# Retention by batch and head pair with tiled fp32 matmuls, and routing through an on-chip slot table

## The chip, the cores and the metric

One core of one Trainium2 chip. The metric is the device time of one execution in microseconds (us). The kernel before takes 367.27 us (median of 3 runs, 363.37 to 367.58); its profiled execution has a span of 363.7 us. Profiles say which state an execution was in; comparisons below are between fast ones unless a sentence says otherwise.

## The reference

```python
# q, k, v: (4 batches, 8 heads, 768 tokens, 64), fp32
state = zeros((B, H, D, D))
for t in range(S):
    state = gamma[h] * state + outer(k[:, :, t], v[:, :, t])
    y[:, :, t] = scale * (q[:, :, t] @ state)
x = y.transpose(0, 2, 1, 3).reshape(3072, 512)

skip_score = x @ w_skip                 # only rows with a score over 0 go to an expert
e_idx  = argmax(x @ w_gate)             # one of 8 experts
gate_w = softmax(x @ w_gate)[e_idx]
out = x
out[active] = x + gate_w * (relu(x @ w1[e]) @ w2[e])   # w1: 512x1024, w2: 1024x512 for each expert
```

For the inputs of this case 1510 of the 3072 rows are active, 133 to 229 per expert.

## The kernel before

Retention works on chunks of 128 tokens, a pair of heads at a time: transposes of q and k, scores, mask, values, and a running state. The two heads of a pair are kept apart by padding K and V with zeros to 128 columns, so every fp32 pass uses the whole array.

```python
    for r in range(SROWS // 128):                    # the scatter buffer is zeroed
        nc.scalar.dma_start(out=xs[r * 128 : (r + 1) * 128, :], in_=xsinit[:, :])
    ...
    def stage_D(s):                                  # scores of two heads, and the state product
        ...
        nc.tensor.matmul(out=ps[:, 0:128], lhsT=KT0z[r][:, :], rhs=QTs[s][:, :], start=True, stop=True)
        nc.tensor.matmul(out=ps[:, 128:256], lhsT=KT1z[r][:, :], rhs=QTs[s][:, :], start=True, stop=True)
        nc.tensor.matmul(out=ps[:, 256:384], lhsT=kg[j][:, pcs], rhs=va[j][:, pcs], start=True, stop=True)
    ...
    def gate_b(j):                                   # 24 times: rows of a chunk go to the buffer
        ...
        nc.gpsimd.indirect_dma_start(
            out=xs[:, :], out_offset=bass.IndirectOffsetOnAxis(ap=dest_i[:, 0:1], axis=0),
            in_=xt[j][:, 0 : XSW], ...)
    ...
    def issue_w2(e, fb, eng):                        # weights: fp32 staging tile, cast by VectorE
        w2st = poolW.tile([128, DM], FP32, tag="w2st", bufs=2, name="w2st")
        nc.sync.dma_start(out=w2st[:, :], in_=moe_w2[e, fb * 128 : (fb + 1) * 128, :])
        ...
        eng.tensor_copy(wbf[:, :], w2st[:, :])
    ...
    # per expert: read 256 rows of xs, transpose, two layers, and for each 128 rows
            nc.gpsimd.indirect_dma_start(
                out=out[:, :], out_offset=bass.IndirectOffsetOnAxis(ap=toks[e][st][:, 0:1], axis=0),
                in_=yout[:, :], ...)
```

## Time and profile before

| stage | us | what sets it |
|---|---|---|
| start | 0 to 30 | ScalarE's queue sits in the issue of the zeroing writes |
| retention and gating | 30 to 254 | TensorE, 87% filled with passes of 0.11 us |
| hole | 254 to 280 | last blocks are gated and routed |
| experts | 280 to 364 | second-layer weights, and at the end the scatters |

In the lines of the profile PE is TensorE, PEld its weight loads, DVE VectorE, ACT ScalarE, POOL GpSimd, SP SyncE. A pass is one weight load with the matmul that uses it; an fp32 matmul takes two passes, an fp32 transpose one. PSUM is the memory that TensorE writes its results to, in banks.

The prediction shows the slices, windows, waits and groups that carry this. One more view is needed to understand what came: GpSimd's last instructions in the order of time (start, duration, instruction, and in brackets how long the engine stood before it and for what):

```profile
348.52 0.97 POOL L463 DMA_INDIRECT out_dram<-yout,tok_i  x1 [3.14 <-DVE yout L459]
352.03 0.97 POOL L463 DMA_INDIRECT out_dram<-yout,tok_i  x1 [2.54 <-DMA out_dram<-yout,tok_i]
355.09 0.97 POOL L463 DMA_INDIRECT out_dram<-yout,tok_i  x1 [2.09 <-DMA out_dram<-yout,tok_i]
358.60 0.97 POOL L463 DMA_INDIRECT out_dram<-yout,tok_i  x1 [2.54 <-DMA out_dram<-yout,tok_i]
```

The reader is to see that each of the last three scatters waits for the scatter before it, and that they stand about 3.4 us apart. In this kernel that binds only at the very end; earlier the scatters come further apart anyway. The prediction did not use these lines, and it should have.

### The profile page before, as it was taken

Reading aid. Unit: us, or ns where it says so; the run is one execution under the profiler, and the core shown is the slowest. Engines: PE = TensorE matmul, PEld = TensorE weight load, DVE = VectorE, ACT = ScalarE, POOL = GpSimd, SP = SyncE. Lnnn points to the kernel's source line nnn. Section 1 sums busy time; section 2 is a strip of 40 time slices with the busy share of each in tenths; the row PEclk is TensorE's granted clock in tenths of the full one; section 3 lists DMA queues with packets and bytes.
Section 4 is the critical chain, followed back from the end, with each engine's and each line's share of the span. In section 5 each row is a group of like instructions: output and inputs, shape, how many; then the busy total and the mean of one; then the engine's idle time right before and its main releaser. Section 6 shows DMA issues by size and latency. Waiting matters only on the chain. (4 is left out here: it accounts for less than half of the span.)

```text
span 363.7 us, 7487 instructions
## 1 busy us (share of the span) xinstructions
PE 298.8 (82%) x2192; PEld 242.4 (67%) x2192; DVE 204.9 (56%) x896; ACT 222.4 (61%) x977; POOL 137.1 (38%) x309
## 2 busy tenths in 40 slices
PE   0005999999999999999999999999524999999860
PEld 0003988888888888888788888888313666666530
DVE  1011667878887878877777777877520224333330
ACT  4006699888887888778778878884102444444310
POOL 8600344545554351454455444441031112222222
PEclk9999999999999999999999999999655999999996
DMA  7999678799969897894987788785416167676611
GB/s 175 263 318 329 190 202 237 220 279 284 240 214 267 241 299 194 239 283 144 234 226 210 204 232 234 214 238 191 142 61 199 45 229 233 228 244 207 205 62 50
DMA packets 101303, 77.31 MB, mean 213 GB/s; under 512 B 79386, under 2 KB 79386, under 8 KB 101264
## 3 DMA queue, kind: packets, MB, share of 16 engines
q1 hardware_dynamic: 95616, 62.96, 61.8%
q0 software_dynamic: 3200, 9.41, 6.9%
q10 hardware_dynamic: 2448, 4.47, 3.7%
q8 instruction: 17, 0.28, 0.3%
q14 instruction: 22, 0.18, 0.2%
HBM read 56.66 MB, written 21.28 MB: 214 GB/s over the span
## 5 line engine op out<-in xcount | busy, mean ns | idle before, releaser
L206 POOL TENSOR_SCALAR kg_all<-k_all,gamk 128x64 f32<-128x64 f32 x192 | 85.6, 471 | 56.6 <-PE atkv_ps L234 27.4
L200 ACT ACTIVATE qg_all<-q_all,gamq 128x64 f32<-128x64 f32 x192 | 55.1, 340 | 21.8 <-DMA xs<-xsinit 21.1
L348 POOL DMA_INDIRECT xs<-x_tile,dest_i x24 | 25.0, 1043 | 96.8 <-ACT QT L220 21.6
L212 PE MATMUL tqk_ps<-ident,qg_all 128*128 128x128 f32 x96 | 28.9, 301 | 30.4 <-ACT V0z L223 30.2
L240 DVE TENSOR_TENSOR ATm<-atkv_ps,maskp 128x256 f32<-128x256 f32 x96 | 40.3, 420 | 21.9 <-PE atkv_ps L234 18.7
L171 DVE CAST w2bf<-w2st 128x512 bf16<-128x512 f32 x64 | 27.7, 434 | 38.5 <-DMA w2st<-in_moe_w_dram 38.3
L446 ACT ACTIVATE hT_sb<-hT_ps 128x256 bf16<-128x256 f32 x64 | 24.5, 384 | 31.8 <-PE hT_ps L441 27.6
L164 DVE CAST w1bf<-w1st 128x512 bf16<-128x512 f32 x64 | 25.5, 437 | 29.9 <-DMA w1st<-in_moe_w_dram 29.9
L232 PE MATMUL atkv_ps<-QT,KT0z 128*128 128x128 f32 x192 | 40.9, 296 | 0.6 <-ACT KT0z L221 0.3
L263 PE MATMUL Y_ps<-V0z,ATm 128*128 128x128 f32 x192 | 38.7, 284 | 1.3 <-DVE ATm L240 1.3
L233 PE MATMUL atkv_ps<-QT,KT1z 128*128 128x128 f32 x192 | 39.2, 287 | 0.0
L234 PE MATMUL atkv_ps<-v_all,kg_all 128*128 128x128 f32 x192 | 39.1, 286 | 0.0
L264 PE MATMUL Y_ps<-V1z,ATm 128*128 128x128 f32 x192 | 37.9, 280 | 0.0
L212 PEld LDWEIGHTS tqk_ps<-ident,qg_all 128*128 128x128 f32 x96 | 13.8, 144 | 35.3 <-issue 31.9
L271 ACT COPY x_tile<-Y_ps 128x128 f32<-128x128 f32 x96 | 25.5, 266 | 19.4 <-PE Y_ps L266 14.3
L441 PE MATMUL hT_ps<-xTe,w1bf 128*128 128x256 bf16 x256 | 35.1, 275 | 0.8
L463 POOL DMA_INDIRECT out_dram<-yout,tok_i x16 | 15.8, 985 | 51.5 <-DMA out_dram<-yout,tok_i 18.7
L441 PEld LDWEIGHTS <-w1bf 128*128 128x128 bf16 x256 | 25.2, 98 | 11.1 <-issue 5.0
L232 PEld LDWEIGHTS atkv_ps<-QT,KT0z 128*128 128x128 f32 x192 | 30.0, 197 | 3.0 <-ACT KT0z L221 2.3
L263 PEld LDWEIGHTS Y_ps<-V0z,ATm 128*128 128x128 f32 x192 | 29.8, 196 | 2.7 <-DVE ATm L240 1.6
L454 PE MATMUL y_ps<-w2bf,hT_sb 128*128 128x512 bf16 x128 | 30.1, 379 | 1.5 <-DVE yout L459 1.5
L291 PE MATMUL gps<-xT_sb,Wc 128*9 128x128 f32 x192 | 29.4, 280 | 2.1 <-DVE xT_sb L279 2.1
(89 smaller groups left out, 641.5 us busy)
## 6 DMA issues: line engine op xcount, KB each, us to landing
w1st<-in_moe_w_dram SPq DMA_DIRECT2D x32, 512.0 KB
w2st<-in_moe_w_dram SPq DMA_DIRECT2D x64, 256.0 KB
q_all<-in_q_dram SPq DMA_DIRECT2D x24, 256.0 KB
k_all<-in_k_dram SPq DMA_DIRECT2D x24, 256.0 KB
v_all<-in_v_dram SPq DMA_DIRECT2D x24, 256.0 KB
out_dram<-x_tile SPq DMA_DIRECT2D x24, 256.0 KB
xs<-xsinit ACTq DMA_DIRECT2D x17, 257.0 KB
xg<-xs SPq DMA_DIRECT2D x16, 257.0 KB
```

Of the source, the lines that this page charges most:

```text
L200: nc.scalar.activation(out=qg[j][:, hc], in_=qa[j][:, hc], func=AF.Copy, bias=0.0, scale=gamq[:, h : h + 1])
L206: nc.gpsimd.tensor_scalar(kg[j][:, hc], ka[j][:, hc], gamk[:, h : h + 1], None, ALU.mult)
L212: nc.tensor.transpose(out=ps[:, 0:128], in_=qg[j][:, pcs], identity=ident[:, :])
L232: nc.tensor.matmul(out=ps[:, 0:128], lhsT=KT0z[r][:, :], rhs=QTs[s][:, :], start=True, stop=True)
L233: nc.tensor.matmul(out=ps[:, 128:256], lhsT=KT1z[r][:, :], rhs=QTs[s][:, :], start=True, stop=True)
L234: nc.tensor.matmul(out=ps[:, 256:384], lhsT=kg[j][:, pcs], rhs=va[j][:, pcs], start=True, stop=True)
L240: nc.vector.tensor_tensor(out=sb[:, :], in0=at_ps[s][:, 0:256], in1=maskp[p][:, :], op=ALU.mult)
L263: nc.tensor.matmul(out=yp[:, 0:128], lhsT=ATm[s][:, 0:128], rhs=V0z[r][:, :], start=True, stop=False)
L264: nc.tensor.matmul(out=yp[:, 0:128], lhsT=ATm[s][:, 128:256], rhs=V1z[r][:, :], start=False, stop=(c == 0))
L291: nc.tensor.matmul(out=gps[0:9, 0:128], lhsT=Wc[:, db * 9 : db * 9 + 9], rhs=xT_sb[:, db * 128 : (db + 1) * 128], start=(db == 0), stop=(d ...
L441: nc.tensor.matmul(out=hT_ps[:, 0:CAP], lhsT=w1bf[e][db][:, fb * 128 : (fb + 1) * 128], rhs=xTes[e][:, db * CAP : (db + 1) * CAP], start=( ...
L454: nc.tensor.matmul(out=y_ps[:, :], lhsT=hTs[fb][:, st * 128 : (st + 1) * 128], rhs=w2bf[e][fb][:, :], start=(fb == 0), stop=(fb == NFB - 1),)
```

## The change

The intent: fewer and cheaper passes in retention, no zeroing, no scatter buffer in memory, no staging and casting of weights. One unit is a batch and a head pair (16 of them, 768 tokens). Partition p of the q and k tiles holds tokens 6p to 6p+5, so that a row is one run of 1536 bytes; GpSimd scales q and k of a whole unit by one multiplication each. Scores use 64 rows of the array for each head, values and state 64 columns, so that two heads can run side by side. Row numbers of each expert's slots are built on chip by small matmuls with one-hot columns, rows are gathered from the output, weights are cast by the DMA itself, and a loop would take over if an expert got more than 256 rows (here it runs zero times). The diff cut to its core:

```diff
-        nc.scalar.dma_start(out=xs[r * 128 : (r + 1) * 128, :], in_=xsinit[:, :])
...
-        nc.sync.dma_start(out=qa[j][:, :], in_=q[b, :, t0 : t0 + C, :].transpose([1, 0, 2]))
+        nc.sync.dma_start(out=qw[i][:, :, :], in_=q[b, hs].rearrange("h (p r) d -> p h (r d)", p=128))
...
-            nc.gpsimd.tensor_scalar(kg[j][:, hc], ka[j][:, hc], gamk[:, h : h + 1], None, ALU.mult)
+            G_.tensor_tensor(o[:, :, :, :], w[i][:, :, :].rearrange("p h (r d) -> p r h d", d=D), sc, ALU.mult)
...
+        o = dst[i][:, :].rearrange("p (t r) -> p r t", r=R)[:, a * HB : (a + 1) * HB, :]
+        A_.copy(out=o, in_=ps[:, :].rearrange("p (r t) -> p r t", r=HB))
...
-        nc.tensor.matmul(out=ps[:, 0:128], lhsT=KT0z[r][:, :], rhs=QTs[s][:, :], start=True, stop=True)
-        nc.tensor.matmul(out=ps[:, 128:256], lhsT=KT1z[r][:, :], rhs=QTs[s][:, :], start=True, stop=True)
+                hp = slice(64 * h, 64 * h + 64)
+                PE.matmul(out=ps[h][:, r * C : (r + 1) * C], lhsT=KT[i][hp, cs], rhs=QT[i][hp, cs], start=True, stop=True)
...
+                PE.matmul(
+                    out=KV[i][64 * h : 64 * h + 64, c * D : (c + 1) * D],
+                    lhsT=Kn[i][:, c, 64 * h : 64 * h + 64], rhs=vn[i][:, h, c, :], start=True, stop=True,
+                )
...
-        nc.sync.dma_start(out=w2st[:, :], in_=moe_w2[e, fb * 128 : (fb + 1) * 128, :])
-        eng.tensor_copy(wbf[:, :], w2st[:, :])
+            G_.dma_start(out=w2b[e][:, :, :], in_=moe_w2[e].rearrange("(a p) d -> p a d", p=128))
...
+    for e in range(E):
+        gather(e, gi)                       # 16 indirect row loads, 128 rows each
+    for e in range(NEARLY, E):              # NEARLY = 4
+        load_w(e, 0, poolE)
+        load_w(e, 1, poolE)
...
+            yo = poolE.tile([128, DM], FP32, tag="yo", bufs=4, name="yo")
+            V_.scalar_tensor_tensor(
+                out=yo[:, :], in0=ps[:, :], scalar=g[:, st, e : e + 1], in1=xg[e, st][:, :], op0=ALU.mult, op1=ALU.add
+            )
+            G_.indirect_dma_start(
+                out=out[:, :], out_offset=bass.IndirectOffsetOnAxis(ap=si[:, st, e : e + 1], axis=0), ...
...
+    NPASS = (N + CAP - 1) // CAP - 1
+    thr_i = poolE.tile([128, NPASS], I32, tag="thr_i", bufs=1, name="thr_i")
+    G_.iota(thr_i[:, :], pattern=[[CAP, NPASS]], base=CAP, channel_multiplier=0)
+    V_.tensor_copy(thr[:, :], thr_i[:, :])  # the test for overflow, once, after all experts
```

> **What bounds the kernel now.** I read four views in this order: the 40 slices of the page, to cut the span into stages; a table of busy time by stretch; the waits; the groups of instructions.
>
> ```profile
> PE   0005999999999999999999999999524999999860
> PEclk9999999999999999999999999999655999999996
> GB/s 175 263 318 329 190 202 237 220 279 284 240 214 267 241 299 194 239 283 144 234 226 210 204 232 234 214 238 191 142 61 199 45 229 233 228 244 207 205 62 50
> ```
>
> Each slice is 9.1 us. Four stages show: no matmul for three slices, 24 full ones (retention and gating), a hole of three slices with a lower clock (the last blocks are routed and scattered), then the experts.
>
> ```profile
> core 0: us, PE busy (x) PEld busy (x) DVE busy (x) ACT busy (x) POOL busy (x), PEclk, DMA share, GB/s
> 100.00:150.00 50.00, 48.84 (x401) 43.60 (x400) 40.66 (x192) 40.85 (x189) 22.63 (x44) 1.00 0.83 243
> 265.00:290.00 25.00, 14.21 (x79) 9.45 (x80) 3.74 (x17) 6.19 (x18) 3.85 (x9) 0.67 0.30 98
> 320.00:363.00 43.00, 29.57 (x184) 17.73 (x182) 12.55 (x24) 13.16 (x37) 10.23 (x13) 0.92 0.47 153
> ```
>
> Retention is set by PE (48.8 of 50 us), though DVE and ACT stand at 41 and the DMA engines at 0.83. In the last 43 us nothing is full: PE 29.6, DMA 0.47. The waits say why, and why the start is empty:
>
> ```profile
> DVE w2bf L171 <- DMA w2st<-in_moe_w_dram: 38.3, 30, 3.4
> PE tqk_ps L212 <- ACT V0z L223: 30.2, 1, 30.2
> ACT qg_all L200 <- DMA xs<-xsinit: 21.1, 1, 21.1
> POOL out_dram L463 <- DMA out_dram<-yout,tok_i: 18.7, 6, 4.8
> ```
>
> PE's 30.2 us before its first transposes go back to ACT, whose queue sits 21.1 us in the issue of 17 zeroing writes of the scatter buffer (4.4 MB) that compete with the first loads. At the end, second-layer weights arrive through two staging tiles and a DVE cast. Four groups give my unit prices:
>
> ```profile
> L206 POOL TENSOR_SCALAR kg_all<-k_all,gamk 128x64 f32<-128x64 f32 x192 | 85.6, 471 | 56.6 <-PE atkv_ps L234 27.4
> L240 DVE TENSOR_TENSOR ATm<-atkv_ps,maskp 128x256 f32<-128x256 f32 x96 | 40.3, 420 | 21.9 <-PE atkv_ps L234 18.7
> L348 POOL DMA_INDIRECT xs<-x_tile,dest_i x24 | 25.0, 1043 | 96.8 <-ACT QT L220 21.6
> L441 PE MATMUL hT_ps<-xTe,w1bf 128*128 128x256 bf16 x256 | 35.1, 275 | 0.8
> ```
>
> The means of PE are latencies. The price of a pass is its spacing: in the order of time around 154 us, one fp32 matmul of 128 columns starts 0.22 us after the last (two weight-load-and-matmul passes of 0.11), an fp32 transpose takes 0.11, eight first-layer bf16 matmuls take 0.9 plus a wait of 0.2, and 14 second-layer ones 3.02 us, 0.216 each.
>
> **What the Trainium skill says.** "TensorE: Matmul & The Clock Gate", Back-to-back issue gap, gives N/2.4 + 2.5 ns warm, 216 ns for 512 columns; the trace has 216. Its Part 3 (Packing small matmuls) measures 3.07x for four row tiles running at once at 512 columns. The kernel before pads K and V with zeros and uses no tile, so its trace neither agrees nor disagrees. "GPSIMD Engine Reference", 3.1, puts a two-input elementwise operation at about 2.6 cycles per element and 4497 ns for 2048, 1.7 us for 768; the trace has only a one-input form, 471 ns for 64, mostly fixed. "DMA: Bandwidth & Descriptors", SWDGE vs HWDGE vs iDMA, says that a cast in flight can be issued from GpSimd only. The trace has no cast in flight.
>
> **The change, part by part.**
>
> *Start.* The scatter buffer, its zeroing and 16 zeroed operand tiles go. The first unit needs q and k, 0.79 MB; at the 175 to 263 GB/s of the first slices that is 3 to 4.5 us plus some 2 us of latency. GpSimd then scales q and k, about 2 us each. First transpose near 9 us instead of about 29: minus 20 us.
>
> *Retention on PE.* The count of passes before, per chunk of 128 tokens: 8 transposes, 24 for the two score products and the state, 22.7 for the output, 4 + 8 for gate transposes and logits, 6 for the rest, 72.7 passes, 8.0 us at 0.11. The stage takes 220 us for 24 chunks, 9.2 each, so PE is 87% filled. After, per unit (batch and head pair, six chunks): 12 + 5 + 6 transposes, 24 passes of scores with 64 rows, 20 of state with 64 columns on both sides, 10 with the state, 24 of values with 64 columns: 101. Sixteen units make 1616 against 1744 before. So almost nothing comes from the count; it must come from the 68 tiled passes of a unit overlapping in pairs. Full overlap would halve them; I take 0.08 us instead of 0.11, since each still needs its weight load: 33 x 0.11 + 68 x 0.08 = 9.1 us per unit.
>
> Waits inside a unit: the second half of the scores reuses the same two PSUM banks, so PE waits for two DVE masks (128x256 costs 0.42, so 384 columns about 0.56 each, an estimate): about 1 us. The state sums are 10 small DVE operations of 0.2 us behind the masks and two copies of 0.56; the state product of the unit, only 12 passes of q later, waits about 1 us more. Changes of tile shape: 0.5. Together 2.5, so 11.6 us per unit, 185 for sixteen. Gate logits and rows are 8 matmuls of 384 columns (0.64 each, some overlapped), 12 short passes and the slot table: about 5 us in each of three batches that lie inside, 15.
>
> Other engines per unit: DVE 4 x 0.56 + 2 x 0.56 + 10 x 0.2 = 5.4 us (the weight casts, 53 us in all, are gone); ACT eight copies of 256 to 384 columns at about 0.5, 3.9; GpSimd two scalings of 1.7 to 2.9, at most 5.8, plus descriptors of one weight load every second unit (512 or 1024 rows at the 8 ns per row that the scatter's 1.04 us for 128 rows gives: 4 to 8 us). All under 11.6. DMA moves 18.9 + 16.8 + 6.3 = 42 MB in 200 us, 210 GB/s, with q and k in 1536-byte runs instead of 256: no bound. Retention ends near 9 + 200 + 5 (last unit's output) = 214 us, against 254.
>
> *The hole.* The before needs 20 us from the last output (254) to the first expert row loads (274). After, logits 3, rows and about 15 small DVE operations at 0.2 with four changes of engine 7, table 3, slot arithmetic 2: 15 us; row numbers at about 230. Then a gather, 1.0 to issue and some 2 to land, and the transposes 2: first expert matmul near 235.
>
> *Experts.* PE: 32 first-layer passes of 0.11, now two blocks per bank and so without the 0.2 waits, 16 of 0.216, 8 short transposes: 7.6 us, eight make 61, so 235 + 61 = 296. But weights of experts 4 to 7 (16.8 MB of fp32 read) are issued on GpSimd behind 16 gathers of 1.04 us: from 247 us. At 300 GB/s (the highest slices have 318 and 329, with fewer bytes in a run) they take 56 us, the last lands at 303, the last second layer adds 4 and the last scatter, its landing and the end 5 (before: last issue at 358.6, end 363.7): 312. The DMA chain is then 11 us longer than PE's. Counts per expert here, worked out from the inputs, are 133 to 229, so the overflow loop runs zero times; its test costs perhaps 2 us beside the last scatters. Prediction on the span 312, and runs lie within 1% of the traced span: 312 us.
>
> **The rivals.**
> 1. Tiles do not overlap (sequencer or mode changes bind). Then 101 x 0.11 = 11.1 us and 3 of waits, 14.1 per unit: plus 40, 350 us. For it: every fp32 pass in the trace stands 0.11 apart, even where only 8 columns stream. Against: the skill's 3.07x.
> 2. Tiles overlap fully: 33 x 0.11 + 34 x 0.11 = 7.4 us, and DVE and the waits show; unit of 9.5, 280 us. The trace's weight load latency of 0.2 us per pass speaks against all of it.
> 3. The cast in flight runs below 300 GB/s. At 150, 16.8 MB take 112 us from 247: 368 us, no gain. Nothing in the trace speaks for or against; an expert wait on weights is what it would show. Faster than 300 it is hidden and PE sets 301.
> 4. Scatters stuck behind the weight descriptors in GpSimd's queue: four output tiles and two banks fill after three experts, and PE stops until the queue is free, up to 20 us more.
>
> **Range and chances.** The start is nearly certain (minus 20), the hole minus 5. Rivals 1 and 3 each raise the time by 40 or more and I give each one chance in six or less in that size; rival 2 has about the same. The range is 278 to 348. Slower than 374 takes both 1 and 3. Chances: faster 0.91, same 0.05, slower 0.04.
>
> **What would show it.** First transpose at 8 to 12 us. Units 11 to 12 us apart, with score and value passes under 0.1 us apart and a PE wait for the score masks. First expert matmul at about 235. Experts 0 to 3 at 7 to 8 us, then waits of PE for DMA of the weights. If units take over 13 us, the tiling step is wrong; if the experts' stage is longer than 85 us, the cast's rate or GpSimd's queue is; if GpSimd is busy over 70% of retention, its scaling was mis-sized and sets the pace.

## The result and the profile after

The changed kernel takes 322.36 us (median of 4 runs, 321.98 to 323.18; all fast) against 366.97 us for the kernel before in the same rounds; the ratio is 0.883, 95% interval 0.877 to 0.889. Ratios here and below are those of the record, from fast runs of the same rounds, so not quite the ratio of the medians quoted. The profiled span is 320.4 us.

The slices of the page (8 us each), to be laid beside those of before:

```profile
PE   1897999966999998999999993087995009889200
PEclk9998999995799999999999995569999557999855
GB/s 215 229 198 250 248 217 213 233 209 295 336 237 102 271 213 70 91 149 101 147 3 0 2 84 114 233 250 182 175 210 209 210 141 49 42 66 54 52 74 28
```

TensorE starts in the first slice and retention is over in the 24th, at 188.5 us. There are two stretches without work: the one expected between retention and the experts, and a second one in the slices at 245 to 265 us. After it the memory traffic is near 50 GB/s to the end. The table of busy time by stretch for the steady part of retention, the second stretch and the last 55 us (columns as in the prediction):

```profile
100.00:150.00 50.00, 48.20 (x543) 39.31 (x541) 29.87 (x106) 25.01 (x43) 14.97 (x10) 1.00 0.48 135
245.00:265.00 20.00, 0.71 (x2) 0.25 (x2) 0.75 (x1) 0.34 (x1) 0.75 (x1) 0.58 0.96 175
265.00:320.00 55.00, 30.96 (x192) 18.47 (x190) 10.77 (x18) 7.16 (x12) 13.88 (x15) 0.81 0.14 53
```

In 100 to 150 us TensorE is as full as before (48.2 of 50), while VectorE and ScalarE fell from 41 to 30 and 25. In the last 55 us nothing is full, not even the DMA (0.14). The waits name what is being waited for:

```profile
DVE yo L485 <- DMA out_dram<-yo,si: 48.7, 12, 20.6
POOL out_dram L488 <- DVE yo L485: 38.9, 2, 35.6
POOL qks L181 <- DMA kw<-in_k_dram: 29.3, 4, 13.8
PE yps L480 <- DVE yo L485: 22.0, 4, 19.4
```

VectorE waits for scatters to free its four output tiles, and TensorE stands 19.4 us for VectorE. (The second line blames VectorE for GpSimd's 35.6 us; VectorE was itself waiting for the scatter.) The third line belongs to the first 80 us: GpSimd waits for k. GpSimd's queue, in the order of time:

```profile
198.74 0.81 POOL L162 DMA_DIRECT2D w1b<-in_moe_w_dram  x1 [40.92 <-PE cnt L512]
199.86 1.09 POOL L446 DMA_INDIRECT xg<-out_dram,gi  x1 [0.31 <-issue]
...
226.13 0.98 POOL L165 DMA_DIRECT2D w2b<-in_moe_w_dram  x1
227.42 1.06 POOL L488 DMA_INDIRECT out_dram<-yo,si  x1 [0.30 <-DVE xb L456]
...
264.25 1.05 POOL L488 DMA_INDIRECT out_dram<-yo,si  x1 [35.60 <-DVE yo L485]
...
313.74 0.97 POOL L488 DMA_INDIRECT out_dram<-yo,si  x1 [2.48 <-DMA out_dram<-yo,si]
```

One weight load is issued at 198.7 us, then sixteen gathers and seven more loads from 199.9 to 227 us. The first scatter goes out at 227.4 and the second only at 264.3. From there fifteen scatters are issued 264.3 to 313.7 us: 14 steps in 49.5 us, 3.5 us each. One link of them in the chain that ended last:

```profile
288.87 2.67 DMA out_dram<-yo,si
291.59 0.51 issue
292.09 0.03 POOLq L488
292.12 0.19 issue
292.32 2.57 DMA out_dram<-yo,si
```

Each scatter lands before the next is issued: 2.6 us from the start of its issue (0.97 us of it the issue) to its landing, and 0.7 to 0.8 us of hand-over. In the packed trace's list of semaphores the scatters wait for the one before them; all write to the output, and nothing in the program says that their rows differ. The Trainium skill ("DMA: Bandwidth & Descriptors", Two DMAs through the same engine are not ordered) says that the only order an author has between two transfers is the first one's completion semaphore. That the scheduler takes these writes for overlapping and orders them so is argued here; x_scratch below tests it. The trace agrees with the page in that each scatter is issued only after the landing of the one before, 3.4 to 3.5 us per scatter, as in the last lines of before. The bytes matter little: worked out from the inputs, the fourth scatter writes 5 rows and its step is 2.96 us, and a scatter of 128 rows takes 3.45.

The groups that answer to those of before, busy time and mean duration of one:

```profile
L216 DVE TENSOR_TENSOR ATm<-atps,maskc 128x384 f32<-128x384 f32 x64 | 32.7, 553 | 67.3 <-PE atps L214 67.3
L193 ACT COPY QT<-tps 128x384 f32<-128x384 f32 x32 | 26.0, 863 | 66.6 <-PE tps L191 66.6
L181 POOL TENSOR_TENSOR qks<-qw,tq 128x768 f32<-128x768 f32 x16 | 23.9, 1495 | 61.1 <-PE tps L191 41.1
```

The mask cost what was estimated (0.56), GpSimd's scaling a little less than the lower estimate (1.7), and ScalarE's copy more (863 ns against 489 ns for its contiguous copy of the same shape).

### The profile page after: what moved, and what is told of

Read it like the earlier page. It is cut to its first block, busy times and chain, and to the rows that moved or that the text cites. A ratio compares the mean times of both kernels' runs of the same rounds, so it can differ in the third digit from the quotient of the medians.

```text
span 320.4 us, 5739 instructions
## 1 busy us (share of the span) xinstructions
PE 240.1 (75%) x2253; PEld 183.8 (57%) x2253; DVE 132.5 (41%) x456; ACT 102.5 (32%) x175; POOL 96.0 (30%) x96
## 5 line engine op out<-in xcount | busy, mean ns | idle before, releaser
L216 DVE TENSOR_TENSOR ATm<-atps,maskc 128x384 f32<-128x384 f32 x64 | 32.7, 553 | 67.3 <-PE atps L214 67.3
L480 PE MATMUL yps<-w2b,hT 128*128 128x512 bf16 x128 | 31.3, 396 | 22.0 <-DVE yo L485 22.0
L191 PE MATMUL tps<-ident,qks 128*128 128x128 f32 x192 | 39.7, 304 | 10.7 <-POOL qks L181 6.5
L193 ACT COPY QT<-tps 128x384 f32<-128x384 f32 x32 | 26.0, 863 | 66.6 <-PE tps L191 66.6
L181 POOL TENSOR_TENSOR qks<-qw,tq 128x768 f32<-128x768 f32 x16 | 23.9, 1495 | 61.1 <-PE tps L191 41.1
L214 PE MATMUL atps<-QT,KT 64*128 64x128 f32 x384 | 38.5, 298 | 0.0
L181 POOL TENSOR_TENSOR qks<-kw,tk 128x768 f32<-128x768 f32 x16 | 24.0, 1498 | 39.4 <-DMA kw<-in_k_dram 29.3
L214 PEld LDWEIGHTS atps<-QT,KT 64*128 64x128 f32 x384 | 32.3, 194 | 5.7 <-issue 2.8
L485 DVE SCALAR_TENSOR_TENSOR yo<-yps,g,xg 128x512 f32<-128x512 f32 x16 | 12.0, 750 | 53.8 <-DMA out_dram<-yo,si 48.7
L469 PE MATMUL hps<-xgT,w1b 128*128 128x256 bf16 x256 | 31.5, 281 | 1.7 <-ACT hT L473 1.7
L247 PE MATMUL yps<-QT,Zb 128*128 128x128 f32 x160 | 30.4, 297 | 0.0
L238 DVE TENSOR_TENSOR Zb<-kvps,Zb 64x64 f32<-64x64 f32 x128 | 28.5, 222 | 4.0
L257 PE MATMUL yps<-ATm,vn 128*64 128x128 f32 x384 | 26.9, 280 | 0.0
```

The costliest lines, as they stand in the source:

```text
L181: G_.tensor_tensor(o[:, :, :, :], w[i][:, :, :].rearrange("p h (r d) -> p r h d", d=D), sc, ALU.mult)
L191: PE.transpose(out=ps[:, r * 128 : (r + 1) * 128], in_=in_, identity=ident[:, :])
L193: A_.copy(out=o, in_=ps[:, :].rearrange("p (r t) -> p r t", r=HB))
L214: PE.matmul(out=ps[h][:, r * C : (r + 1) * C], lhsT=KT[i][hp, cs], rhs=QT[i][hp, cs], start=True, stop=True)
L216: V_.tensor_tensor(out=ATm[i][:, h, a * HB : (a + 1) * HB, :], in0=ps[h][:, :].rearrange("p (c t) -> p c t", c=HB), in1=maskc[:, :].unsque ...
L238: V_.tensor_tensor(z, kv, Zb[i % 2][c - 1][hp, hp], ALU.add)
```

## The experiments

The theory after the first look (A): the end is set by sixteen scatters in a chain, which starts late because the first scatter stands behind seven weight loads in GpSimd's one DMA queue; retention's gain comes from tiles that overlap, less some 10 us in which the early weight loads starve q, k and v. Rivals: the 19.4 us stop of TensorE is what costs; the bandwidth is what costs; the unit's pace is not set by TensorE. Twelve kernels ran, each with three rounds against the kernel before.

| run | us (median) | ratio | correct rows |
|---|---|---|---|
| changed kernel | 322.36 | 0.883 | yes |
| x_inplace | 321.18 | 0.878 | yes |
| x_scratch | 305.29 | 0.834 | no, on purpose |
| x_scratch_inplace | 299.06 | 0.820 | no, on purpose |
| x_scratch_early_test | 286.45 | 0.787 | no, on purpose |
| x_late_sp | 307.89 | 0.841 | yes |
| x_late_weights | 312.54 (fast runs 309.02 and 310.96) | none given | yes |
| x_untiled_scores | 324.88 | 0.892 | no, on purpose |
| x_untiled_all | 351.59 | 0.967 | no, on purpose |
| x_chunk_rows | 335.60 | 0.909 | yes |
| b_zero_sp | 402.26 | 1.105 | yes |
| x_best | 280.75 | 0.767 | yes |
| x_best_gate | 281.53 | 0.774 | yes |

The kernel before had medians of 363.35 to 365.71 us in these rounds. The comparison with the reference is loose: it told "correct" of the three kernels that send the experts' rows elsewhere, so it proves little about routed rows.

**x_inplace: does the stop of TensorE cost anything?** The output is written over the gathered rows, so sixteen tiles stand in for four.

```diff
-            yo = poolE.tile([128, DM], FP32, tag="yo", bufs=4, name="yo")
+            yo = xg[e, st]
```

> The output tile of an expert is written over its gathered rows, so the four output buffers are in effect sixteen; the result stays right. Theory A (queue and chain: the first scatter lands only when the seven weight loads ahead of it in GpSimd's DMA queue have drained, and each of the 16 scatters then waits for the one before to land, 3.4 us each): the stop of TensorE of 19 us in the experts' stage vanishes or is below 3 us, but the time stays at 318 to 326 us. Theory B (the four output buffers that stop TensorE are the loss): about 303 us.

Measured: 321.18 us. The wait of TensorE for VectorE's output tiles is gone from the list, and TensorE is done at 272 us instead of 298.5, yet the scatters stand at 226.3, then 262.8 to 312.3 us as before. The last lines of TensorE and of GpSimd:

```profile
268.44 3.62 PE L480 MATMUL yps<-w2b,hT 128*128 128x512 bf16 x16
312.30 0.97 POOL L488 DMA_INDIRECT out_dram<-xg,si  x1 [2.48 <-DMA out_dram<-xg,si]
```

The stop was a symptom: taking it away alone is worth 1 us, no more than the spread of the runs.

**x_scratch: are the scatters chained?** Each scatter writes to a buffer of its own, so no one waits for another (the result is wrong on purpose).

```diff
+    scr = [poolD.tile([N, DM], FP32, name=f"scr{n}") for n in range(2 * E)]
...
-                out=out[:, :], out_offset=bass.IndirectOffsetOnAxis(ap=si[:, st, e : e + 1], axis=0),
+                out=scr[2 * e + st][:, :], out_offset=bass.IndirectOffsetOnAxis(ap=si[:, st, e : e + 1], axis=0),
```

> Each of the 16 scatters writes a DRAM buffer of its own, so none waits for the one before; the result is wrong on purpose (routed rows keep the retention output). Theory A: the scatters still land only at about 263 us of the span, TensorE still stops for 19 us, but the chain after it is gone: the end is TensorE's, about 298 us, 22 less than the changed kernel. Theory B: 322 us, no change, since the buffers are the same. Theory C (the weight reads fill all DMA engines and slow every scatter): 322 or a little less.

Measured: 305.29 us, 17 us less, where 298 was expected. The stop of TensorE remained (16.8 us), and now it does cost, for TensorE sets the end.

**x_scratch_inplace: both.**

> Both edits together, result wrong on purpose. Theory A: TensorE never stops for outputs, the last weights land near 263 us, the last expert ends near 270 and the span near 278: 44 us less than the changed kernel. Theory B: 303 us. Theory C: above 300 us.

Measured: 299.06 us, far from 278. In place of the old stop there is a new one, as the waits show:

```profile
DVE thr L512 <- issue: 19.4, 1, 19.4
PE hps L471 <- DVE xgT L462: 13.6, 1, 13.6
```

TensorE waits for VectorE's copy of transposed rows, which stands in VectorE's queue behind `thr`, a cast for the overflow test; `thr` needs an iota that stands in GpSimd's queue behind a blocked scatter. Eleven numbers of a test that belongs to the end hold up the matmuls in the middle, because the scheduler put them ahead of what TensorE needs: VectorE stands 19.4 us at `thr`, with the copy behind it. (In the changed kernel itself the test holds nothing up: its iota ran at 228.5 us and its cast at 242.1 us without a wait. The stop comes from the order that the scheduler chose for the runs with private buffers.)

**x_scratch_early_test: is that it?** As the last, with the iota and its cast moved to the constants at the start.

```diff
+    thr_i = poolC.tile([128, NPASS], I32, name="thr_i")          # among the constants
+    G_.iota(thr_i[:, :], pattern=[[CAP, NPASS]], base=CAP, channel_multiplier=0)
+    V_.tensor_copy(thr[:, :], thr_i[:, :])
```

> Each scatter to its own buffer (wrong result on purpose), outputs over the gathered rows, and the constants of the overflow test made at the start instead of behind the scatters on GpSimd. Theory A: the 13.6 us that the PE waited in the run with private buffers and in-place outputs came from VectorE's cast waiting for GpSimd's small iota behind blocked scatters: they go, and the time falls from 299 to 283-288 us. Rival: something else behind the same stop (weights, PSUM banks): 296 us or more, with the wait of PE on the weights or on VectorE still over 8 us.

Measured: 286.45 us, as expected; once the experts run, no wait of TensorE is longer than 1.9 us. With private buffers and the weight loads drained, scatters go out 1.3 us apart, not 3.4:

```profile
262.80 0.98 POOL L496 DMA_INDIRECT scr<-xg,si  x1 [4.13 <-DMA scr<-xg,si]
264.08 0.98 POOL L496 DMA_INDIRECT scr<-xg,si  x1 [0.30 <-issue]
265.37 0.98 POOL L496 DMA_INDIRECT scr<-xg,si  x1 [0.30 <-issue]
```

So with the chain, the tiles and the test gone, the experts' stage is 36 of the 322 us shorter. The three do not add up one by one, since each hides behind the one before, and the test became a stop only once the chain was gone.

**x_late_sp: queue or bandwidth?** Weights of the last four experts come in fp32 over SyncE's queue through three staging tiles, cast by VectorE and ScalarE in turn; outputs in place; scatters to the real output.

```diff
-    for e in range(NEARLY, E):
-        load_w(e, 0, poolE)
-        load_w(e, 1, poolE)
+            stg = poolE.tile([128, F], FP32, tag="wst", bufs=3, name="wst")   # 16 per expert
+            nc.sync.dma_start(out=v, in_=srcw)
+            (V_.tensor_copy or A_.copy)(dst, v)
```

> Weights of experts 4 to 7 are loaded as fp32 on SyncE's queue through three staging tiles and cast by VectorE and ScalarE, output over the gathered rows; scatters keep their chain; the result stays right. The same bytes are read from memory at the same time. Theory A: the first scatter lands about 3 us after its issue near 220 us, two per expert of 7.4 us fit the chain of 3.4 us each, and the time is about 283 us. Theory C (bandwidth, not the queue): scatters take far more than 3.4 us while weights stream, and the time is above 305 us.

Measured: 307.89 us, above the 305 of theory C and 25 us above the 283 of theory A. By the time alone the bandwidth would be the cause; GpSimd's queue shows that it is only part of it (its first two scatters and its last):

```profile
224.28 1.03 POOL L488 DMA_INDIRECT out_dram<-xg,si  x1 [5.16 <-DVE w2b L511]
230.80 1.01 POOL L488 DMA_INDIRECT out_dram<-xg,si  x1 [5.50 <-DVE xb L456]
...
295.70 0.98 POOL L488 DMA_INDIRECT out_dram<-xg,si  x1 [2.48 <-DMA out_dram<-xg,si]
```

The second scatter goes out 6.5 us after the first, not 36.8 us: the queue was what blocked it. But while weights stream, the first eight steps are 5.2 to 6.8 us instead of 3.4 (the next one, to 274.9, is 3.5), so traffic beside them stretches the chain: a scatter then lands 4.4 to 5.3 us after its issue instead of 2.6. Both theories hold a part: the queue is worth the start, the bandwidth takes some of it back.

**x_late_weights: the early starvation.** Each of the eight early weight loads is made to wait for a unit's K, from unit 3 on, by a one-column copy into its tile.

```diff
-        if i % 2 == 1 and wjobs and i < NU:
-            load_w(*wjobs.pop(0), poolW)
+        if i >= 3 and wjobs and i < NU:
+            load_w(*wjobs.pop(0), poolW, KT[i][:, 0:1])
...
+                V_.tensor_copy(w1b[e][:, 0, 0:1], gate)
```

> The loads of the first four experts' weights are held back, one per unit from unit 3 on, so that they don't all run in the first 80 us. Theory A: the waits of GpSimd for q/k (29 us in all) and of PE for v and q/k in the first 85 us come from these loads; retention ends 8-14 us earlier (175-181 us instead of 188.5) and the time is 308-315 us. Rival: the unit's pace is set by other things and the loads only shift the loss: retention ends at 186 us or later, 320 us or more.

Measured: 312.54 us (two of the four runs fell in the slow state, so no ratio was given; the fast ones are 309.02 and 310.96, inside theory A's range). GpSimd's waits for q and k in the first 90 us fell from 40.7 us (29.3 for k, 11.4 for q) to 4.3 us:

```profile
POOL qks L185 <- DMA qw<-in_q_dram: 2.6, 2, 1.8
POOL qks L185 <- DMA kw<-in_k_dram: 1.7, 1, 1.7
```

From the first unit's K copy to the last one's takes 156.5 us instead of 167.2, and the last gate copy starts at 180.6 us instead of 191.3. In the changed kernel the loads were issued with no wait before them, so all eight had been issued by 44 us.

**x_untiled_scores: what do row tiles give?** Scores over all 128 rows (wrong on purpose).

```diff
-... lhsT=KT[i][hp, cs], rhs=QT[i][hp, cs], start=True, stop=True)
+... lhsT=KT[i][:, cs], rhs=QT[i][:, cs], start=True, stop=True)
```

> The scores alone are done with all 128 rows instead of two 64-row tiles (wrong result on purpose; same number of passes, same shapes). If tiles overlap in pairs and PE sets the pace of retention, a unit's 24 score passes go from 0.059 to 0.11 us apart: 1.2 us per unit, 16 units: 19-20 us more, 337-344 us. Rival (the pace is set by the masks on VectorE and the copies, and PE has slack): under 328 us. If row tiles gave nothing: 322 us with score passes at 0.059 still.

Measured: 324.88 us; the expectation of 337 to 344 was wrong, and the rival is nearer. Four units with their share of gating take 43.2 us instead of 41.7, 0.4 us per unit. In the unit near 138 us the first twelve score passes took 0.87 us tiled and 1.34 us whole, but the second twelve took 1.33 and 1.46: they reuse the same two PSUM banks and wait for VectorE's masks either way. From the first score to the last it is 2.91 against 3.39 us, a saving of 0.48 where twice the first 0.47 would be 0.94. So the tiles do overlap, and half of what they save goes into that wait.

**x_untiled_all: what do all tiles give?** Scores, values and state on the whole array (wrong on purpose).

```diff
-                    out=KV[i][64 * h : 64 * h + 64, c * D : (c + 1) * D],
-                    lhsT=Kn[i][:, c, 64 * h : 64 * h + 64], rhs=vn[i][:, h, c, :], start=True, stop=True,
+                    out=KV[i][:, c * D : (c + 1) * D],
+                    lhsT=Kn[i][:, c, :], rhs=vn[i][:, h, c, :], start=True, stop=True,
...
-                    lhsT=vn[i][:, h, c, :], rhs=ATm[i][:, h, c, :], ...
+                    lhsT=vn[i][:, h, min(c, NCH - 2) : min(c, NCH - 2) + 2, :].rearrange("p c d -> p (c d)"), rhs=...
```

> Scores, state and values all on the whole array (wrong result on purpose, same number of passes). If the tiles are what retention's speed rests on: values 24 passes of a unit from 0.061 to 0.11 us, state 20 from 0.036 to 0.11, scores as measured alone (0.4 us per unit): 3.1 us per unit, 16 units: 45-50 us more, retention ends at 233-240 us and the time is 362-374 us, about that of the kernel before. Rival (the unit is paced by the engines around PE, as the run with untiled scores suggests): under 345 us.

Measured: 351.59 us, 29 us more than the changed kernel. That is neither the expected 362 to 374 nor the rival's under 345: the expected 45 to 50 us were too many. TensorE in the order of time, first in the changed kernel (start, duration to the end of the group, shape of the weights, passes):

```profile
138.20 0.94 PE L214 MATMUL atps<-QT,KT 64*128 64x128 f32 x12
141.37 0.80 PE L226 MATMUL kvps<-vn,Kn 128*64 128x64 f32 x20
145.60 1.53 PE L257 MATMUL yps<-ATm,vn 128*64 128x128 f32 x24
147.06 0.77 PE L203 MATMUL tps<-ident,KT 128*128 128x128 f32 x5
```

and then in this run:

```profile
139.17 1.50 PE L214 MATMUL atps<-QT,KT 128*128 128x128 f32 x12
142.67 2.34 PE L226 MATMUL kvps<-vn,Kn 128*128 128x64 f32 x20
148.37 1.84 PE L257 MATMUL yps<-ATm,vn 128*128 128x128 f32 x15
```

The 24 value passes take 1.46 us from their first start to the next group's (147.06 - 145.60), 0.061 each, against about 0.11 when whole; the 20 state passes go from 0.11 to under 0.04. Four steady units with gating take 52.4 us instead of 41.7 (from one K copy to the one four units on), 2.7 us per unit, near the 3.1 expected. Sixteen times 2.7 would be 43; the total moved by 29, because the first 85 us are held by data in the changed kernel and the extra passes partly fit into those waits: the ninth unit's K copy comes only 4.0 us later (107.5 against 103.5), the last one's 24.4. Before, 220 us for sixteen units' worth of work make 13.75 us per unit; after it is 10.4, and 13.1 without tiles. So tiling carries 2.7 of the 3.3 us. The edit does two things at once for state and values, though: no two passes overlap, and each weight load has 128 columns instead of 64 (192 against 138 to 146 ns). Only the scores, whose loads stayed at 194 ns, show the overlap alone.

**x_chunk_rows: the six-token rows.** q and k in runs of 256 bytes, a token of each chunk per partition; the copies of the transposes are then contiguous.

```diff
-        nc.sync.dma_start(out=qw[i][:, :, :], in_=q[b, hs].rearrange("h (p r) d -> p h (r d)", p=128))
+                nc.sync.dma_start(
+                    out=t[:, h, :].rearrange("p (c d) -> p c d", d=D),
+                    in_=srcq[b, 2 * p + h].rearrange("(c p) d -> p c d", p=128),
+                )
...
-        A_.copy(out=o, in_=ps[:, :].rearrange("p (r t) -> p r t", r=HB))
+        A_.copy(out=dst[i][:, a * HW : (a + 1) * HW], in_=ps[:, :])
```

> The six-token rows of q and k undone: 256-byte runs, one token of each chunk per partition, and ACT's copies of the transposes are contiguous. Theory A (row shape is worth little): 316-328 us; ACT's copy of 384 columns falls from 863 to about 490 ns, the first transpose comes 1-3 us later. Rival (small runs take DMA time that the weights and q/k need in the first 80 us): 330 us or more, with longer GpSimd waits for q/k.

Measured: 335.60 us, two runs slow and two fast (329.85 and 333.95, mean 331.9), so the rival. ScalarE's copies fell from 863 to 479 ns as expected, and a steady unit is only 0.15 us shorter for it (41.1 us for four). The loss is in the first 60 us: the third unit's K copy comes at 56.0 us instead of 32.5. From the waits in 20 to 60 us (the profiled execution is a slow one, but this stop is in its first 60 us and not a matter of some per cent):

```profile
POOL qks L185 <- DMA qw<-in_q_dram: 20.6, 2, 20.1
PE gps L291 <- DMA Wc<-in_moe_w_skip_dram: 19.4, 1, 19.4
```

So the long rows buy time from DMA, and pay for it with a slower ScalarE that had slack. That the short runs as such are what costs is likely but not shown, for the edit also makes four transfers out of two. How much of it would remain with the weight loads held back was not run.

**b_zero_sp: the start alone.** The kernel before, with its zeroing writes issued by SyncE.

```diff
-        nc.scalar.dma_start(out=xs[r * 128 : (r + 1) * 128, :], in_=xsinit[:, :])
+        nc.sync.dma_start(out=xs[r * 128 : (r + 1) * 128, :], in_=xsinit[:, :])
```

> The kernel before with nothing changed but the queue that issues the 17 zeroing writes of its scatter buffer: SyncE's instead of ScalarE's. If the empty start (first transposes at 29 us) comes from ScalarE's queue sitting in their issue: first transposes at 10-14 us and 345-352 us in all. Rival (the writes hold back the first loads by bandwidth, or ScalarE's other start-up work is long): first transposes after 20 us, 358 us or more.

Measured: 402.26 us, 37 us slower. The first transposes of before and of this run:

```profile
30.16 0.45 PE L212 MATMUL tqk_ps<-ident,qg_all 128*128 128x128 f32 x1 [30.16 <-ACT V0z L223]
```

```profile
8.96 0.45 PE L212 MATMUL tqk_ps<-ident,qg_all 128*128 128x128 f32 x1 [8.96 <-ACT V0z L223]
```

The reason for the empty start is confirmed, 21 us of it. But the scheduler, given one different queue, put most of the program in another order (TensorE's differs from its 91st instruction on), and in 70 to 150 us TensorE runs 391 passes instead of 642; it waits again and again for the scaling of k. The total therefore says nothing about the start, and why the new order is so much worse was not followed up.

**x_best: what was learnt, in a correct kernel.** Six experts' weights are loaded during retention, one load per unit from unit 2 on; a seventh expert's go into the slots that q and k leave free; the eighth's two loads stand among the first gathers, none ahead of a scatter. The overflow constants are made at the start, outputs are in place, and retention's outputs are stored per unit (which, with one buffer of transposed outputs fewer, makes room for two more experts' weights).

> Correct version from what was learnt: weights of six experts loaded during retention, one load per unit from unit 2 on; those of a seventh in the slots that q and k leave free; one expert's two loads after the first gathers; nothing ahead of the scatters in GpSimd's queue; outputs over the gathered rows; overflow constants at the start; outputs of retention stored per unit. Theory A (chain of 16 scatters of 3.4 us from the first one at about 210 us): 265-280 us, no stop of PE over 8 us. Rival (the loads make retention DMA-bound, or scatters stay slow): 290 us or more.

Measured: 280.75 us, ratio 0.767 (0.760 to 0.775), 0.75 us outside the expected range. It beats both kernels. GpSimd's first two scatters and its last:

```profile
218.02 1.04 POOL L521 DMA_INDIRECT out_dram<-xg,si  x1 [3.63 <-DVE xg L518]
221.60 1.01 POOL L521 DMA_INDIRECT out_dram<-xg,si  x1 [2.54 <-DMA out_dram<-xg,si]
...
271.86 0.98 POOL L521 DMA_INDIRECT out_dram<-xg,si  x1 [2.50 <-DMA out_dram<-xg,si]
```

Fifteen steps in 53.8 us, 3.6 each: the chain still sets the end, only it starts at 218 instead of 264.

**x_best_gate: the last expert's loads behind the first gathers.** One weight load stood ahead of the first gather, in the changed kernel too, and its rows came 8 us after their issue.

```diff
-            load_w(7, e, poolE)
+            load_w(7, e, poolE, g[:, 0, e : e + 1])
```

> The previous best version with one difference: the two weight loads of the last expert are held until the row numbers are ready, so that the first expert's two gathers stand ahead of them in GpSimd's queue. If that one load of weights is what the first gathers' rows wait for (9.5 us of PE before the first expert): first expert matmul at 196-198 us instead of 202.3, first scatter at 213-214 us instead of 218, 272-277 us in all. Rival (the rows of the second expert then wait instead, and the first scatter comes no earlier): 279 us or more.

Measured: 281.53 us, no better than x_best; the rival. The first rows were cast 3.4 us after their gather's issue, but the later gathers then met the loads, the last went out at 216.9 us instead of 213.4, and the first scatter at 221.6. These times are from a profile of the slow state, in which the row numbers also came 1.5 us later, so what they suggest, that the wait moved by a few instructions and stayed, is not shown; that nothing was gained is, by the fast runs (279.78 to 283.96 us).

## Why the prediction was right or wrong

The time, 312 predicted and 322.36 measured, lies inside the range of 278 to 348, and the direction was right. The sum was right by luck: retention ended 25.5 us early, the hole was 1.3 us longer, and the experts' stage took 109.6 us instead of 77, 32.6 more; together these are the 8.4 us by which the span of 320.4 exceeds 312. The step that fails is the end: the prediction lets the last weights set it, and a chain of scatters set it. Its own sign, an experts' stage longer than 85 us, did name GpSimd's queue beside the cast's rate.

- **Start: right in kind.** First transpose predicted near 9 us, measured 6.5, before the 8 to 12 given as its sign. The prediction's "about 29" for the kernel before is 30.2 in its own lines.
- **Retention: mechanism right, size off.** Predicted 11.6 us per unit and 15 us for three batches of gating, 12.5 per unit in all; measured 10.4 in the steady part. The term that was mis-sized is the tiled pass, taken as 0.08 us: values measured 0.061, state under 0.04, scores 0.07 until the mask wait binds. The 0.5 us for changes of tile shape was a guess that no run measures. The prediction's 1.7 us for a scaling was its own estimate, in proportion to the page's figure; measured 1.495. Rival 2, full overlap, came nearer: 9.5 us and the same share of gating make 10.4. x_untiled_all shows that tiling carries the gain, 2.7 us per unit, overlap and shorter weight loads together.
- **"DMA: no bound": wrong in the first 85 us.** The average of 210 GB/s was no guide, because the early weight loads are all issued by 44 us. x_late_weights shows the cost, 10.7 us of retention. Retention ended at 188.5 us where 214 was predicted.
- **Hole: right in sum, wrong in its parts.** Row numbers came 10.5 us after retention instead of 16, first matmul 11.8 us after that instead of 5; of those, 8 are the first gather's landing, behind one weight load. In sum 22.3 against 21.
- **GpSimd's issue of a weight load: wrong, and harmless.** Predicted 4 to 8 us by rows, measured 0.80 to 0.99.
- **Rate of the cast in flight: wrong.** 300 GB/s was assumed and the last weights at 303 us. GpSimd's transfers take one of eight semaphores in turn (109 to 116 in the packed trace), and each waits for the last use of its own. In x_scratch_inplace the second to the eighth scatter so wait for one of the seven loads each, and their issues at 231.5, 236.9, 242.0 and so on to 262.0 count the loads off: one load of 2.1 MB of fp32 per 5.1 us, about 410 GB/s. The last landed near 262 us, not 303, and no wait of TensorE for weights is in the changed kernel's list. The step "the DMA chain is then 11 us longer than PE's" fails.
- **Scatters: the missing term.** The prediction has "the last scatter, its landing and the end 5". Rival 4 foresaw the queue and the stop ("up to 20 us more"; 19.4 measured), but put the cost in the stop. x_inplace shows that the stop costs 1 us. What sets the end is that the last fifteen scatters follow each other at 3.4 to 3.5 us, from 264 us on: 264.3 + 14 x 3.5 = 313.3, and 7 us for the last landing and the end, 320. The lines at the end of the kernel before already showed the spacing.

What stays open: whether a correct kernel can scatter without the chain (no way was found to tell the scheduler that the rows differ), and the order that made b_zero_sp slow.

## What to carry to other kernels

When a change makes a stage faster, look for the serial chains that the slower stage had hidden: here a scatter every 3.4 us was invisible while experts took 10 us, and became the end of the kernel. Put nothing long ahead of a short transfer that others wait for in the same queue, and nothing small that belongs to the end ahead of work that another engine waits for. A wait that an engine reports is worth removing only if that engine is on the chain that ends last; take the wait away alone before believing it.

## What the Trainium skill lacked or had wrong

- "DMA: Bandwidth & Descriptors" says that GpSimd's path has one queue, but not what it costs: a scatter issued behind seven weight loads held its successor back 36.8 us (227.4 to 264.3), against 6.5 us with the weights on another queue.
- The same page fits the time of one transfer on GpSimd's path by its size, which makes an estimated 2.6 us for 256 KB, as measured here from issue to landing; it has no figure for scatters, nor for a chain of them: up to 128 rows of 2 KB, each after the other's landing, take 3.4 to 3.5 us, 2.96 with 5 rows, and with weights streaming beside them 5.2 to 6.8.
- The same page's bandwidth table has no cast in flight: 2.1 MB of fp32 read per 5.1 us, about 410 GB/s, for 1 MB written. The issue of such a load of 512 or 1024 rows takes 0.80 to 0.99 us, no more than that of 128 indirect rows (0.97 to 1.2).
- "TensorE: Matmul & The Clock Gate", Part 3, names 512 columns wherever it gives the size of a measured packing, and nothing for fp32. For fp32 and two tiles: 0.061 us per pass of 128 columns instead of 0.11, and 0.036 instead of 0.11 for 64 columns, a factor of three, which two tiles alone do not explain; the weight loads were shorter too, and no run here takes the two apart.
- "GPSIMD Engine Reference", 3.1, was close: an estimated 1.7 us by its cycles for a two-input operation on 768 elements, 1.495 measured.
- "SBUF — State Buffer", Door 1: The DMA port swizzle, says that accesses that cross to a new 16-byte line pay a penalty, without a size for ScalarE: a copy of 384 columns written at a stride of 24 bytes took 863 ns, contiguous 479 to 489, about 1 ns per element.
